# Transposes of the folded spectrum moved into the same round's other small matmuls, in front of them

## The chip, the cores and the metric

The kernel runs on one core of one Trainium2 chip. The metric is the device time of one execution in microseconds; lower is better. The three runs of the kernel before took 1345.86, 1345.98 and 1347.0 us.

## The reference

Three stages follow each other on an input of 4 batches x 3136 positions x 256 channels, all in float32:

```python
y = irfft(rfft(x, axis=1) * (filt_r + 1j * filt_i), n=3136, axis=1)      # filter along the positions
m = real(fft(fft(y, axis=1), axis=2))                                    # spectrum along both axes
u = y + m
u = u + relu(norm(u) @ w1a) @ w2a                                        # 256 -> 1024 -> 256
u = u + relu(norm(u) * g @ w1b) @ w2b                                    # again, with a gain
```

`norm` subtracts the mean over the channels and divides by the root of the variance plus 1e-6.

## The kernel before

**The products.** Almost all of TensorE's work is the two channel products. The tokens come in 25 units U of 512 tokens (the last has 256), each with two layers. A block (U, layer) has eight steps, so there are 400 steps. A step has a first product (`w1_step`, line 904: 12 matmuls of 256 columns, from `xth` and `xtl`, the high and low half of the normalised tokens) and a second (`w2_step`, line 931: 8 matmuls with `hh`, then 4 with `hl`). Between them `w1_evict` makes `hh` (ScalarE, line 913) and `hl` (VectorE, line 914). The main loop (lines 1110 to 1121) does, for step i: the first product of step i + 2, then all that the table `at` holds for step i, then the second product of step i, then the eviction of step i + 2. So whatever `at` calls on TensorE interrupts the products at one fixed place, after line 904 of step i + 2 and ahead of line 931 of step i. Every engine works through its instructions in the order written here.

**The filter beside them.** Batch 0's filter runs ahead of the products. For batches 1 to 3 it runs in pieces under the products of the batch before: `over_p(b)` (first transform), then `over_q(b)`, a generator whose `yield`s divide it into ticks. Its main loop runs over rounds j = 0 to 9, each with two ticks, in two neighbouring steps (`slots`; `first` puts the tick ahead of all else at its step). A round does, for frequency pair group j and the group before it:

- `into(j)`: 64-row matmuls from `gr` into two PSUM banks R and I (line 267, `ps<-gr`);
- `back(j - 1)`: 64-row matmuls from the filtered `y` into two banks V (line 267, `ps<-y`), which ScalarE copies to `vst` (line 609; in round 1 line 605, and VectorE's 606);
- `filt(j, R, I)`: four VectorE multiplications with the filter (line 573), then two GpSimd additions (lines 574 and 575) that make `y`;
- `turn_z(j - 1)`: four transposes of `z` by TensorE (line 618; two in the last round), copied by ScalarE to `zt` (line 625);
- `half(j)`: GpSimd folds `y` into `z` (line 584, two instructions), ScalarE sets its first column (line 585);
- `store`, `sign`, `load_g`, `load_f`: the output of V, a sign for the next filter, the next loads.

The first four rounds' steps of batch 1 are 25, 30, 34 and 36; rounds 5 and 6 stand at 50 and 52. In batches 2 and 3 rounds are five or more steps apart, at steps that leave 4, 9 or 14 when divided by 16. At those that leave 4 the tick is followed by the split of a coming block's `xtl` (line 825, VectorE; line 824, ScalarE, makes `xth`).

**Normalisation.** `ln_ticks` makes `xth` and `xtl`. Most blocks turn the tokens through DRAM (`TURN`); the first units, the last ones and each batch's first unit turn them on TensorE (lines 828 to 838): per half k of the channels four transposes (line 831), a copy by ScalarE and a split by VectorE, and a `yield`. Of these, eight blocks have the two halves at two different steps: layer 0 of units 6, 12, 18 and 24, layer 1 of units 1, 2, 23 and 24. In the others both ticks fall into one step.

PSUM has eight banks, all from one pool (`bank`); two hold the sums of the second product.

Of the kernel before, what the change touches and what calls it, by code (L numbers as in the profile page):

```python
# [13 lines left out]
ACTF = mybir.ActivationFunctionType  # L14
ALU = mybir.AluOpType
# [168 lines left out]
def spectral_mlp_kernel(ctx: ExitStack, tc, x, ff, ff0, cst, w1a, w2a, gln, w1b, w2b, out):  # L184
# [43 lines left out]
    def bank(k=1):  # L228
        t = banks.tile([128, 512], F32, tag="b", name="ps")
        return t if k == 1 else t.rearrange("p (a d) -> p a d", a=k)  # L230

    def f32(ap):
        return ap.bitcast(F32)
# [28 lines left out]
    def split(src, hi, lo, lo_eng=None):  # L262
        nc.scalar.activation(out=hi, in_=src, func=ACTF.Copy)
        (lo_eng or nc.vector).tensor_tensor(out=lo, in0=src, in1=f32(hi), op=ALU.subtract)
# [264 lines left out]
    def over_q(b):  # L529
# [17 lines left out]
        def into(j):  # L547
            g = g_raw.pop((b, j))
            R, I = (bank(2) for _ in range(2))
            f2 = const("f2")  # L550
            if j == 0:
                for r, o, n in ((0, R, "f2a"), (64, I, "f2a")):
                    quarter(o[:, 0], 0, const(n), r, NI, g[:, 0])
                for r, o, n in ((0, I, "f2b"), (64, R, "f2b")):
                    quarter(o[:, 0], 64, const(n), r, NI, g[:, 0])
                for r, o in ((0, R), (64, I)):
                    quarter(o[:, 1], 0, f2, r, NI, g[:, 1])
                for r, o in ((0, I), (64, R)):
                    quarter(o[:, 1], 64, f2, r, NI, g[:, 1])
            else:  # L560
                n = len(steps_of(j))
                for c in range(2):
                    for r, o in ((0, R), (64, I)):
                        quarter(o[:, :n], 64 * c, f2, r, NI, g[:, c:2 * n:2])
            return R, I
# [22 lines left out]
        def back(j):  # L588
            n = len(steps_of(j))
            y = ys.pop(j)  # L590
            V = [bank(2) for _ in range(2)]
            if j == 0:
                for c in range(2):
                    for h in range(2):
                        quarter(V[h][:, 0], 64 * c, const("i1z", 64 * c, 64), 64 * h, NQ, y[:, 0, c])
                for c in range(2):
                    quarter(V[0][:, 1], 64 * c, const("i1", 64 * c, 64), 0, NQ, y[:, 1, c])
            else:
                for c in range(2):
                    for h in range(2):  # L600
                        quarter(V[h][:, :n], 64 * c, const("i1", 64 * c, 64), 64 * h, NQ, y[:, :n, c])
            st = stg.tile([128, 4, D], F32, tag="st", name="vst")
            vst[j] = st
            if j == 0:
                nc.scalar.activation(out=st[:, :2], in_=V[0], func=ACTF.Copy)
                nc.vector.tensor_tensor(out=st[:, 0], in0=V[1][:, 0], in1=st[:, 0], op=ALU.add)
            else:
                for h in range(2):
                    nc.scalar.activation(out=st[:, h:2 * n:2], in_=V[h][:, :n], func=ACTF.Copy)
# [21 lines left out]
        sign(0)  # L631
        yield
        for j in range(NDUO + lag):
            RI = into(j) if j < NDUO else None
            if j >= lag:
                back(j - lag)
            if RI:
                filt(j, *RI)
            yield
            if j >= lag:  # L640
                turn_z(j - lag)
            i = j - lag + 1
            if 0 <= i < NDUO:
                half(i)
            if j >= lag:
                store(j - lag)
            if j + 1 < NDUO:
                sign(j + 1)
            if j + 2 < NDUO:
                load_g(b, j + 2)  # L650
            nxt = j + 2
            if nxt < NDUO:
                load_f(b, nxt)
            yield
# [107 lines left out]
    def ln_ticks(U, layer, sets=None):  # L762
        n = tiles(U)
        u = u_of[U]
        xs = {}
        turn = (U, layer) in TURN
        xall = None
        for tl in sets or [slice(0, n)]:
            ts = range(n)[tl]
            scaled = U < 2 or turn  # L770
            st = sm.tile([128, 4, 6], F32, tag="bs", name="bs")
            mv = sm.tile([128, 4, 2], F32, tag="mv", name="mv")
            rs = sm.tile([128, 4], F32, tag="rs", name="rs")
            for t in ts:
                nc.vector.bn_stats(out=st[:, t], in_=u[:, t])  # L775
            for t in ts:
                nc.vector.bn_aggr(out=mv[:, t], in_=st[:, t])
            nc.vector.tensor_scalar_add(out=rs[:, tl], in0=mv[:, tl, 1], scalar1=EPS)  # L778
            nc.gpsimd.tensor_tensor(out=rs[:, tl], in0=rs[:, tl], in1=mhalf[:, tl], op=ALU.pow)  # L779
            yield  # L780
            if scaled:
                nb = sm.tile([128, 4], F32, tag="nb", name="nb")
                nc.vector.scalar_tensor_tensor(out=nb[:, tl], in0=mv[:, tl, 0], scalar=-1.0, in1=rs[:, tl],  # L783
                                               op0=ALU.mult, op1=ALU.mult)
            xall = xall or xnp.tile([128, 4 * D], F32, tag="xn", name="xn")
            for t in ts:
                xs[t] = xall[:, t * D:t * D + D]
                if turn:
                    xs[t] = xall.rearrange("p (j k t a) -> p j k t a", j=4, k=2, t=4)[:, :, :, t]
                    nc.scalar.activation(out=xs[t], in_=u[:, t].rearrange("p (k a j) -> p j k a", k=2, j=4),  # L790
                                         func=ACTF.Identity, scale=rs[:, t:t + 1], bias=nb[:, t:t + 1])
                    if t % 2:
                        yield
                    continue
                if scaled:
                    nc.scalar.activation(out=xs[t], in_=u[:, t], func=ACTF.Identity, scale=rs[:, t:t + 1],
                                         bias=nb[:, t:t + 1])
                    continue
                nc.vector.tensor_scalar(out=xs[t], in0=u[:, t], scalar1=mv[:, t, 0:1], scalar2=rs[:, t:t + 1],
                                        op0=ALU.subtract, op1=ALU.mult)  # L800
        if turn:


            nc.vector.transpose(out=xall, in_=xall)
            xd = xdp.tile([128, 4 * D], F32, tag="xd", name="xd")
            nc.sync.dma_start(out=xd, in_=xall)
        yield
        xt = {s: xtp.tile([128, 2, 512], F32R, tag="x" + s, name="xt" + s) for s in "hl"}
        xt_of[U, layer] = xt
        w = n * 128  # L810
        if turn:
            src = xd.rearrange("(i a) (j c r) -> i (a j) c r", i=4, j=4, c=8)
            dst = f32(xt["l"]).rearrange("p k (t i r) -> i p (k t) r", t=4, i=4)
            for i in range(4):
                nc.sync.dma_start(out=dst[i], in_=src[i])
            yield
            for k in range(2):
                h, l = (xt[s][:, k] for s in "hl")
                if layer:
                    nc.scalar.activation(out=h, in_=f32(l), func=ACTF.Copy, scale=g_sb[:, k:k + 1])  # L820
                    nc.vector.scalar_tensor_tensor(out=l, in0=f32(l), scalar=g_sb[:, k:k + 1], in1=f32(h),
                                                   op0=ALU.mult, op1=ALU.subtract)
                else:
                    nc.scalar.activation(out=h, in_=f32(l), func=ACTF.Copy)
                    nc.vector.tensor_tensor(out=l, in0=f32(l), in1=f32(h), op=ALU.subtract)  # L825
                yield
            return
        for k in range(2):
            ps = bank()
            for t in xs:  # L830
                nc.tensor.transpose(ps[:, t * 128:t * 128 + 128], xs[t][:, k * 128:k * 128 + 128], ident)  # L831
            if layer:
                nc.scalar.activation(out=xt["h"][:, k, :w], in_=ps[:, :w], func=ACTF.Copy, scale=g_sb[:, k:k + 1])
                nc.vector.scalar_tensor_tensor(out=xt["l"][:, k, :w], in0=ps[:, :w], scalar=g_sb[:, k:k + 1],  # L834
                                               in1=f32(xt["h"][:, k, :w]), op0=ALU.mult, op1=ALU.subtract)
            else:
                split(ps[:, :w], xt["h"][:, k, :w], xt["l"][:, k, :w])
            yield

    alone = False  # L840
# [108 lines left out]
    with tc.manual_schedule():  # L949
# [60 lines left out]
        k = 0  # L1010
# [197 lines left out]
```

## Time and profile before

| | |
|---|---|
| three runs, us | 1345.86, 1345.98, 1347.0 (median 1345.98) |
| the profiled execution, us | 1346.94 |
| its span from the first to the last instruction, us | 1345.2 |
| TensorE, matmuls | 1317.5 us busy, 98% of the span |
| VectorE | 796.5 us, 59% |
| ScalarE | 616.9 us, 46% |
| GpSimd | 270.5 us, 20% |
| mean granted TensorE clock | 0.992 |

The profiled execution lies 0.96 us above the median; 1.74 us of it lie outside the span. TensorE's matmuls overlap in the records, so its busy time says that it is the bound, not how much of it is lost; that is read from the starts of its instructions in the timeline.

### The profile page before, as it was taken

To read this page: it belongs to the slowest core of one execution; us is meant where nothing else is said; L and a number is where in the kernel's file an instruction comes from. 1 tells how busy PE (TensorE), PEld (TensorE's weight loads), DVE (VectorE), ACT (ScalarE), POOL (GpSimd) and SP (SyncE) were. 2 spreads that over 40 slices of the span, in tenths; PEclk is the share of its full clock that TensorE was granted. 3 is DMA by queue.
4 is the path that set the end of the run, shared out by engine and by line. 5 is a ranking of instruction groups with operands and counts; after the bars stand their busy time and mean duration, and the time that the engine had idled before them with its cause. 6 is when DMAs were issued, how large, how long until landed. Compare 5 with 4: busy or idle time off the path is not lost.

```text
span 1345.2 us, 27766 instructions
## 1 busy us (share of the span) xinstructions
PE 1317.5 (98%) x11221; PEld 1211.0 (90%) x11221; DVE 796.5 (59%) x1643; ACT 616.9 (46%) x1205; POOL 270.5 (20%) x277
## 2 busy tenths in 40 slices
PE   8969999999999999999999999999999999999998
PEld 6527998899989989999988999999999999999998
DVE  5968875666454666656454665656555555465453
ACT  5646544454435444544434544545434443444322
POOL 1763012332040222212032221312000000000000
PEclk9979999999999999999999999999999999999999
DMA  8754323443544634623353535534221413332200
GB/s 315 253 192 146 101 92 76 154 115 86 134 140 136 153 91 116 165 62 95 89 170 104 161 106 123 147 81 111 56 64 48 95 34 77 80 83 45 64 17 24
DMA packets 214920, 147.97 MB, mean 110 GB/s; under 512 B 163516, under 2 KB 187196, under 8 KB 214792
## 3 DMA queue, kind: packets, MB, share of 16 engines
q1 hardware_dynamic: 198056, 117.36, 33.6%
q10 hardware_dynamic: 16736, 28.84, 5.9%
q8 instruction: 88, 1.44, 0.5%
q14 instruction: 40, 0.33, 0.1%
HBM read 87.71 MB, written 58.46 MB: 109 GB/s over the span
## 4 chain that ended last, share of the span: by engine, by line
PE 92%; DVE 4%; DMA 1%; ACT 1%; issue 1%; POOL 1%; SPq 0%; ACTq 0%; DVEq 0%; POOLq 0%
PE ps L931 39%; PE ps L904 38%; PE ps L267 7%; PE ps L731 2%; PE ps L320 2%; PE ps L365 1%; PE ps L426 1%; PE ps L618 1%; PE ps L831 1%; PE ps L382 0%; DVE hl L914 0%; DMA vd<-vst 0%; DVE bs L775 0%; DMA gd<-gst 0%; DVE wm L873 0%
## 5 line engine op out<-in xcount | busy, mean ns | idle before, releaser
L914 DVE SCALAR_TENSOR_TENSOR hl<-ps,hh 128x512 fp32r<-128x512 f32 (+1 forms) x400 | 269.5, 675 | 328.6 <-ACT hh L913 323.1
L913 ACT ACTIVATE hh<-ps 128x512 fp32r<-128x512 f32 (+1 forms) x400 | 233.6, 586 | 359.1 <-PE ps L931 314.9
L904 PE MATMUL ps<-xth,w1a 128*128 128x256 f32 x1568 | 243.0, 276 | 0.0
L904 PE MATMUL ps<-xth,w1b 128*128 128x256 f32 x1568 | 242.5, 276 | 0.0
L931 PE MATMUL ps<-w2a,hh 128*128 128x256 f32 x1568 | 219.5, 282 | 0.0
L931 PEld LDWEIGHTS ps<-w2a,hh 128*128 128x128 f32 x1568 | 194.4, 189 | 27.0 <-issue 24.6
L931 PE MATMUL ps<-w2b,hh 128*128 128x256 f32 x1568 | 215.1, 279 | 0.5 <-ACT hh L913 0.5
L904 PEld LDWEIGHTS ps<-xth,w1a 128*128 128x128 f32 x1568 | 207.9, 188 | 1.3 <-issue 1.3
L904 PEld LDWEIGHTS ps<-xth,w1b 128*128 128x128 f32 x1568 | 207.5, 188 | 0.0
L931 PEld LDWEIGHTS ps<-w2b,hh 128*128 128x128 f32 x1568 | 193.2, 188 | 15.4 <-issue 13.8
L779 POOL TENSOR_TENSOR rs<-rs,mhalf 128x4 f32<-128x4 f32 (+1 forms) x51 | 50.9, 997 | 591.6 <-DVE rs L778 506.6
L904 PE MATMUL ps<-xtl,w1a 128*128 128x256 f32 x784 | 154.6, 277 | 0.0
L904 PE MATMUL ps<-xtl,w1b 128*128 128x256 f32 x784 | 154.3, 276 | 0.0
L790 ACT ACTIVATE xn<-u,nb,rs 128x256 f32<-128x256 f32 x152 | 120.3, 840 | 49.5 <-DVE nb L783 47.6
L931 PE MATMUL ps<-w2b,hl 128*128 128x256 f32 x784 | 122.0, 277 | 1.3 <-DVE hl L914 1.3
L931 PE MATMUL ps<-w2a,hl 128*128 128x256 f32 x784 | 121.9, 277 | 1.1 <-DVE hl L914 1.1
L904 PEld LDWEIGHTS ps<-xtl,w1a 128*128 128x128 f32 x784 | 118.7, 188 | 0.6 <-DVE xtl L825 0.6
L904 PEld LDWEIGHTS ps<-xtl,w1b 128*128 128x128 f32 x784 | 118.7, 188 | 0.2 <-DVE xtl L834 0.2
L931 PEld LDWEIGHTS ps<-w2b,hl 128*128 128x128 f32 x784 | 103.8, 188 | 2.1 <-DVE hl L914 2.1
L931 PEld LDWEIGHTS ps<-w2a,hl 128*128 128x128 f32 x784 | 104.2, 188 | 1.3 <-DVE hl L914 1.3
L935 DVE TENSOR_TENSOR u<-ps,u 128x512 f32<-128x512 f32 x98 | 63.1, 685 | 44.4 <-PE ps L931 44.4
L775 DVE BATCH_NORM_STATS2 bs<-u 128x6 f32<-128x256 f32 x196 | 68.6, 411 | 0.0
(146 smaller groups left out, 1449.1 us busy)
## 6 DMA issues: line engine op xcount, KB each, us to landing
xd<-xn SPq DMA_DIRECT2D x38, 512.0 KB
xtl<-xd SPq DMA_DIRECT2D x152, 128.0 KB
fc<-in_ff SPq DMA_DIRECT2D x34, 512.0 KB
vr<-vd SPq DMA_DIRECT2D x48, 256.0 KB
out<-u SPq DMA_DIRECT2D x24, 512.0 KB
vd<-vst ACTq DMA_DIRECT2D x21, 512.0 KB
xr<-in_x SPq DMA_DIRECT2D x18, 512.0 KB
gd<-gst ACTq DMA_DIRECT2D x36, 256.0 KB
```

What stands on the lines that cost most here:

```text
L267: nc.tensor.matmul(out=o[c:c + 64], lhsT=lhs[r:r + k], rhs=rhs[r:r + k], **{"start": True, "stop": True, **kw})
L320: nc.tensor.matmul(out=o, lhsT=cf[at // 512][:k, at % 512:at % 512 + w], rhs=rhs[:k, c0:c1], start=start, stop=stop)
L365: nc.tensor.matmul(out=ps[:, o:o + 128], lhsT=x[:, j, a * 128:a * 128 + 128], rhs=cf[0][:, :128], start=True, stop=True)
L731: nc.tensor.matmul(out=ps[a][:, eo], lhsT=lhs, rhs=cs[eo][r], start=eo == 1 and i == 0, stop=False, skip_group_check=True)
L775: nc.vector.bn_stats(out=st[:, t], in_=u[:, t])
L779: nc.gpsimd.tensor_tensor(out=rs[:, tl], in0=rs[:, tl], in1=mhalf[:, tl], op=ALU.pow)
L790: nc.scalar.activation(out=xs[t], in_=u[:, t].rearrange("p (k a j) -> p j k a", k=2, j=4), func=ACTF.Identity, scale=rs[:, t:t + 1], bias= ...
L904: nc.tensor.matmul(out=ps[:, c:c + 256], lhsT=w[:, a, k, m * 128:m * 128 + 128], rhs=xt[s][:, k, c:c + 256], start=i == 0, stop=i == len(t ...
L913: nc.scalar.activation(out=h[:, :n], in_=ps[:, :n], func=ACTF.Relu)
L914: nc.vector.scalar_tensor_tensor(out=l[:, :n], in0=ps[:, :n], scalar=0.0, in1=f32(h[:, :n]), op0=ALU.max, op1=ALU.subtract)
L931: nc.tensor.matmul(out=o[:, t % 2], lhsT=a[:, t * 128:t * 128 + 128], rhs=w[:, b, m], start=m == 0 and i == 0 and t % 2 == 0, stop=m == 7 ...
L935: nc.vector.tensor_tensor(out=u[:, t - 1:t + 1], in0=o, in1=u[:, t - 1:t + 1], op=ALU.add)
```

## The change

In a round, the transposes of the group before (`turn_z`) leave the second tick and go to the first, ahead of `back`; `back` now stands ahead of `into`. In the normalisation, every unit but the first turns both halves of the channels in one tick: eight transposes into two banks, then the two pairs of copies and splits. The second tick of those that had one is then empty.

```diff
         for j in range(NDUO + lag):
-            RI = into(j) if j < NDUO else None
-            if j >= lag:
-                back(j - lag)
-            if RI:
-                filt(j, *RI)
-            yield
             if j >= lag:
                 turn_z(j - lag)
+                back(j - lag)
+            if j < NDUO:
+                filt(j, *into(j))
+            yield
             i = j - lag + 1
             if 0 <= i < NDUO:
                 half(i)
...
-        for k in range(2):
-            ps = bank()
-            for t in xs:
-                nc.tensor.transpose(ps[:, t * 128:t * 128 + 128], xs[t][:, k * 128:k * 128 + 128], ident)
-            if layer:
...
-            else:
-                split(ps[:, :w], xt["h"][:, k, :w], xt["l"][:, k, :w])
+        for ks in ((0, 1),) if U else ((0,), (1,)):
+            out_k = {k: bank() for k in ks}
+            for k, ps in out_k.items():
+                for t in xs:
+                    nc.tensor.transpose(ps[:, t * 128:t * 128 + 128], xs[t][:, k * 128:k * 128 + 128], ident)
+            for k, ps in out_k.items():
+                if layer:
...
+                else:
+                    split(ps[:, :w], xt["h"][:, k, :w], xt["l"][:, k, :w])
             yield
```

From here on the changed kernel's lines below 631 carry other numbers (the transposes of line 831 are at line 830, `xtl` of line 825 at line 823).

TensorE at round 6 of batch 1 (steps 52 and 53), before: `gr` is read by `into`, `y` by `back`, `z` by `turn_z`.

```order
L904 MATMUL ps<-xtl,w1b 128x256 x2
L267 MATMUL ps<-gr,con 64x512 x4
L267 MATMUL ps<-y,con 64x512 x4
L931 MATMUL ps<-w2b,hh 128x256 x8
L931 MATMUL ps<-w2b,hl 128x256 x4
L904 MATMUL ps<-xth,w1b 128x256 x4
L904 MATMUL ps<-xtl,w1b 128x256 x2
L904 MATMUL ps<-xth,w1b 128x256 x4
L904 MATMUL ps<-xtl,w1b 128x256 x2
L618 MATMUL ps<-con,z 128x128 x4
L931 MATMUL ps<-w2b,hh 128x256 x8
```

And in the changed kernel:

```order
L904 MATMUL ps<-xtl,w1b 128x256 x2
L618 MATMUL ps<-con,z 128x128 x4
L267 MATMUL ps<-y,con 64x512 x4
L267 MATMUL ps<-gr,con 64x512 x4
L931 MATMUL ps<-w2b,hh 128x256 x8
```

The trace shows each of the 64-row matmuls of line 267 as two instructions, so x4 here is x8 there. The transposes stand one step earlier, and `into` stands last in its interruption instead of first. There are 27 such rounds with `turn_z`, 24 of them with an `into`.

ScalarE in the round at step 41 of batch 1, before (the `zt` copies stand in the second tick):

```order
L913 ACTIVATE hh<-ps 128x512
L609 ACTIVATE vst<-ps 128x2x256 x2
L913 ACTIVATE hh<-ps 128x512
L625 ACTIVATE zt<-ps 128x8x49
L585 ACTIVATE z<-y 128x4
L545 DMA vd<-vst 128x1024
```

And in the changed kernel:

```order
L913 ACTIVATE hh<-ps 128x512
L625 ACTIVATE zt<-ps 128x8x49
L609 ACTIVATE vst<-ps 128x2x256 x2
L913 ACTIVATE hh<-ps 128x512
L585 ACTIVATE z<-y 128x4
L545 DMA vd<-vst 128x1024
```

The copy of the transposes moves ahead of the copies of V; the store's DMA keeps its place. VectorE, GpSimd and the DMA queue of SyncE keep their order in the rounds.

## Rows read from the trace of the kernel before

**Rows 1.** The page, part 1: busy time, share of the span, instructions.
```profile
PE 1317.5 (98%) x11221; PEld 1211.0 (90%) x11221; DVE 796.5 (59%) x1643; ACT 616.9 (46%) x1205; POOL 270.5 (20%) x277
```

**Rows 2.** Timeline, TensorE, step 132: start us, us, engine, line, operation, tiles, form, count.
```profile
552.24 1.09 PE L267 MATMUL ps<-gr,con 50*64 50x512 f32 x8
553.15 1.04 PE L267 MATMUL ps<-y,con 49*64 49x512 f32 x8
554.12 1.18 PE L931 MATMUL ps<-w2b,hh 128*128 128x256 f32 x8
...
556.95 0.60 PE L618 MATMUL ps<-con,z 128*128 128x128 f32 x4
557.31 1.17 PE L931 MATMUL ps<-w2b,hh 128*128 128x256 f32 x8
558.31 0.62 PE L931 MATMUL ps<-w2b,hl 128*128 128x256 f32 x4
...
559.90 0.39 PE L904 MATMUL ps<-xtl,w1a 128*128 128x256 f32 x2
...
560.13 1.07 PE L931 MATMUL ps<-w2b,hh 128*128 128x256 f32 x8
...
561.03 0.62 PE L931 MATMUL ps<-w2b,hl 128*128 128x256 f32 x4
```

**Rows 3.** Timeline, TensorE, the last round of batch 1 with two transposes.
```profile
343.08 0.38 PE L618 MATMUL ps<-con,z 128*128 128x128 f32 x2
...
344.23 0.62 PE L931 MATMUL ps<-w2b,hl 128*128 128x256 f32 x4
```

**Rows 4.** Timeline, TensorE, batch 0: transposes followed by 64-row matmuls.
```profile
80.58 0.44 PE L454 MATMUL ps<-con,z 128*128 128x128 f32 x2 [2.39 <-ACT z L477]
80.95 1.41 PE L267 MATMUL ps<-xf,con 64*64 64x512 f32 x8
```

**Rows 5.** Timeline, VectorE, step 132; then the view of line 825 alone.
```profile
553.38 0.69 DVE L573 TENSOR_TENSOR y<-ps,fc 128x512 f32<-128x512 f32 x1 [1.05 <-PE ps L267]
...
555.88 3.02 DVE L825 TENSOR_TENSOR xtl<-xtl,xth 128x512 fp32r<-128x512 f32 x2
```
```profile
L825 DVE TENSOR_TENSOR xtl<-xtl,xth x36: 680/1319/1782, 239.2 to 1244.5; 128x512 fp32r<-128x512 f32 x36
```

**Rows 6.** Timeline, batch 1, rounds 5 and 6 (steps 50 to 52).
```profile
290.22 1.43 POOL L584 TENSOR_TENSOR z<-y 128x254 f32<-128x254 f32 x2
```
```profile
292.50 0.59 ACT L913 ACTIVATE hh<-ps 128x512 fp32r<-128x512 f32 x1
```
```profile
291.45 1.09 PE L267 MATMUL ps<-gr,con 50*64 50x512 f32 x8
```

**Rows 7.** Timeline, batch 1, rounds 2 and 3 (steps 34 to 38).
```profile
233.33 1.43 POOL L584 TENSOR_TENSOR z<-y 128x254 f32<-128x254 f32 x2
...
235.57 1.09 PE L267 MATMUL ps<-gr,con 50*64 50x512 f32 x8
...
239.21 3.08 DVE L825 TENSOR_TENSOR xtl<-xtl,xth 128x512 fp32r<-128x512 f32 x2
...
244.00 0.69 DVE L914 SCALAR_TENSOR_TENSOR hl<-ps,hh 128x512 fp32r<-128x512 f32 x1
...
244.74 0.74 PE L931 MATMUL ps<-w2b,hl 128*128 128x256 f32 x4 [0.21 <-DVE hl L914]
```

**Rows 8.** Timeline, batch 1, round 1 (steps 30 to 33).
```profile
216.04 0.68 DVE L573 TENSOR_TENSOR y<-ps,fc 128x512 f32<-128x512 f32 x1
...
221.45 1.19 PE L931 MATMUL ps<-w2b,hh 128*128 128x256 f32 x8 [0.32 <-ACT hh L913]
...
224.66 1.19 PE L931 MATMUL ps<-w2b,hh 128*128 128x256 f32 x8 [0.20 <-ACT hh L913]
```

**Rows 9.** Timeline, batch 2, step 110 and after: ScalarE and TensorE.
```profile
488.09 0.59 ACT L913 ACTIVATE hh<-ps 128x512 fp32r<-128x512 f32 x1
...
490.01 1.07 PE L931 MATMUL ps<-w2b,hh 128*128 128x256 f32 x8
```

More of the change, by code (lines that the diff above doesn't have):

```diff
@@ L827, in ln_ticks @@
             return
-        for k in range(2):
-            ps = bank()
-            for t in xs:
-                nc.tensor.transpose(ps[:, t * 128:t * 128 + 128], xs[t][:, k * 128:k * 128 + 128], ident)
-            if layer:
-                nc.scalar.activation(out=xt["h"][:, k, :w], in_=ps[:, :w], func=ACTF.Copy, scale=g_sb[:, k:k + 1])
-                nc.vector.scalar_tensor_tensor(out=xt["l"][:, k, :w], in0=ps[:, :w], scalar=g_sb[:, k:k + 1],
-                                               in1=f32(xt["h"][:, k, :w]), op0=ALU.mult, op1=ALU.subtract)
-            else:
-                split(ps[:, :w], xt["h"][:, k, :w], xt["l"][:, k, :w])
+        for ks in ((0, 1),) if U else ((0,), (1,)):
[5 more added lines that the diff above has]
+                if layer:
+                    nc.scalar.activation(out=xt["h"][:, k, :w], in_=ps[:, :w], func=ACTF.Copy, scale=g_sb[:, k:k + 1])
+                    nc.vector.scalar_tensor_tensor(out=xt["l"][:, k, :w], in0=ps[:, :w], scalar=g_sb[:, k:k + 1],
+                                                   in1=f32(xt["h"][:, k, :w]), op0=ALU.mult, op1=ALU.subtract)
+                else:
+                    split(ps[:, :w], xt["h"][:, k, :w], xt["l"][:, k, :w])
             yield
```

## Prediction

> **What bounds the kernel now.** I read the busy times first, then TensorE's timeline around the interruptions, then the timelines of the engines that feed it. TensorE is busy for 98% of the span [rows 1], no other engine for more than 59%. The timeline shows that this is not an average over idle and full stretches: once the filter runs under the products, TensorE goes from product to small matmul and back without waiting, but for a few rows that carry an idle time in brackets. So two things count: how long TensorE itself takes for what it issues, and whether anything it needs comes later than before. The change touches both.
>
> **TensorE's own saving.** Eight products take 560.13 to 561.03 = 0.90 us [rows 2]. With four transposes ahead of them, it is 556.95 to 558.31 = 1.36 us, so that interruption costs 0.46 us. With two transposes it is 343.08 to 344.23 = 1.15 us [rows 3], so 0.25 us. Two more transposes cost 0.21 us, one about 0.11 us. Four at 0.11 us are 0.43 to 0.44 us, and what is left, 0.02 to 0.03 us, is the price of the interruption as such. That alone is what a joined interruption can give back; the transposes stay. The changeover that the trace lacks at full load is transposes to 64-row matmuls. The nearest row is from batch 0: two transposes and the changeover take 80.58 to 80.95 = 0.37 us after a wait [rows 4]; less two paces of 0.11 us, the changeover adds 0.15 us at most beyond a transpose's own pace. A round also begins with a changeover today, so the difference lies between 0.05 us worse and 0.05 us better. I take 0.02 us saved for each of 27 rounds and as much for each of the eight border blocks: 35 x 0.02 = **0.7 us saved**, with ends at 1.8 us saved and 1.4 us lost (27 x 0.05).
>
> Here a rule speaks for the change. The Trainium skill (TensorE: Matmul & The Clock Gate, "Back-to-back issue gap") gives a lone matmul of N columns a spacing of N / 2.4 + 2.5 ns at the full clock, so 56 ns for 128 columns; an estimate by it is 0.22 us for four transposes, and 0.24 us of the 0.46 us would be the interruption. The same section says that the formula leaves out the weight loads. The rows decide against it here: the third and fourth transpose cost as much as the first two.
>
> The border blocks also move the second half's copy and split one to three steps earlier. Their inputs are ready at the first half's step, so nothing new is waited for; the copies join other work on ScalarE and VectorE, which have room. I cost that at nothing.
>
> **What the filter loses.** Now `into` comes after the transposes and `back`. The four multiplications (line 573) wait for it. At step 132 they start at 553.38, 1.14 us after `into` began at 552.24 [rows 2, 5]. In the changed kernel `into` begins later by four transposes (0.44 us) and by `back`, as long as the 0.91 us from 552.24 to 553.15: **1.35 us later**. All that follows them on VectorE moves too, and so do GpSimd's additions and `half`. TensorE's own schedule hardly moves: 0.44 us more in this interruption, 0.46 us less in the next. So every slack below 1.35 us behind `filt` becomes a wait of TensorE.
>
> *Six rounds ahead of an `xtl` split* (steps 116, 132, 148, 212, 228, 244). The two splits of line 825 follow the multiplications directly, 555.88 to 558.90 [rows 5]; TensorE wants the second at 559.90 [rows 2]. Slack 1.00 us, delay 1.35 us: 0.35 us of waiting, and some 0.05 us to restart. 6 x 0.4 = **2.4 us lost**. The ends: one split takes 0.68 us at least and 1.78 us at most [rows 5], so the pair could take 1.36 us, which leaves no wait, or 3.56 us, 0.5 us more each: 0 to 5.4 us.
>
> The long splits run beside GpSimd's additions. The Trainium skill (SBUF — State Buffer, "Who interferes with whom") says that a VectorE instruction with two SBUF inputs and a GpSimd instruction that reads SBUF shut each other out for a whole instruction, the later one waiting. The spread of line 825 from 0.68 to 1.78 us agrees; as both streams are moved by the same 1.35 us, I leave the overlap as it is.
>
> *Batch 1, round 5 to 6.* The rounds stand two steps apart. GpSimd's two instructions of `half` end at 291.65 [rows 6]; they move by 1.35 us, so `z` is complete at 293.0. The transposes now head round 6, due about 0.1 us ahead of today's 291.45 as they need no changeover; the second of them, due at 291.45, needs the second `half`. That is a wait of **1.6 us**; `turn_z` used to come one step later. All eight PSUM banks are then in use, and bank I is the one that the transposes just left, free when ScalarE has copied it. ScalarE's `hh`, 292.50 to 293.09 today [rows 6], waits behind a normalisation that waits for the same GpSimd queue, so it ends near 294.45, and a copy of half a microsecond near 294.95; `into` wants I at 293.0 + 0.33 (the transposes) + 0.2 (changeover) + 0.91 (`back`) = 294.45 and so waits **0.45 us**. The split of `xtl`, later still, adds 0.15 us. Together **2.2 us lost**.
>
> *Batch 1, round 2 to 3.* The same, without the other GpSimd work between. `half` ends at 234.76 [rows 7], so at 236.1 in the change; the second transpose is due at about 235.57: **0.6 us**. The multiplications of round 3 follow 1.9 us later than today, the splits end at 242.29 + 1.9 = 244.2, and `hl`, which VectorE makes next but for the statistics of a normalisation, ends at 244.69 + 1.9 = 246.6. TensorE waits for that `hl` already today, at 244.74, so it moves by the whole **1.9 us**, the 0.6 us included.
>
> *Four rounds ahead of a normalisation* (steps 110, 126, 206, 222). Here the multiplications delay the bias, the bias two ScalarE normalisations, and these `hh`: 488.09 to 488.68, wanted at 490.01 [rows 9], slack 1.33 us. With 1.35 us it is just late, and the next `hh` too; I take 0.2 us each: **0.8 us lost**, 0 to 2 us.
>
> *Round 1 of batch 1 gains.* VectorE must first finish line 606, which waits for `back`; so the multiplications start only at 216.04 [rows 8]. With `back` first, `into` is done at about 215.57, 0.47 us earlier, and the copies of the transposes leave ScalarE's queue between. TensorE idles 0.32 and 0.20 us for `hh` behind it; I take **0.5 us saved**. The remaining rounds (first, last, and those that leave 9 by 16) have more slack than 1.35 us behind them, or no `filt`.
>
> The store's DMA, the loads on SyncE's queue and GpSimd's order keep their places; `store` waits for copies of V that now come earlier.
>
> **The sum.** -0.7 + 2.4 + 2.2 + 1.9 + 0.8 - 0.5 = +6.1 us. On the profiled execution, 1346.94 us, that is 1353.0; on the median of the runs, 0.96 us lower, 1345.98 + 6.1 = **1352.1 us**, 0.45% slower.
>
> **The rivals.** *The delay is absorbed.* If line 825 runs without GpSimd beside it, and `half` overlaps better than the rows say, no new wait reaches TensorE and only 0.7 us of saving remains: 1345.3. For it: VectorE idles over a third of the time. Against: rows 5 to 7 stand in the very stretches where it does not. 0.17.
>
> *The interruption is dearer than I read, and the change is faster.* After transposes the eight products take 557.31 to 558.31 = 1.00 us, 0.10 us more than otherwise [rows 2]. If that were the interruption's and not the last transpose's, 35 x 0.10 = 3.5 us come back: 1342.5, as long as the waits stay below that. The point that decides is whether the joined rounds cost less than 2.34 us (1.88 + 0.46). Against it speaks the comparison of two and four transposes. By the formula of the Trainium skill named above, the estimate would be 35 x 0.24 = 8.4 us. 0.07.
>
> *Banks run short in every round.* A joined interruption takes five banks where it took four. If not two but all 24 rounds waited some 0.5 us, as in round 6, the cost would be 12 us on top of the sum less the 0.45 us counted: 1364. Against it: only in the two close rounds does the order make a bank wait for an eviction of the same interruption. 0.07.
>
> **The numbers.** My forecast has 0.69. A measurement of this kernel can tell about 0.2%, 2.7 us, from no change. The forecast and the bank rival are slower: 0.76. The absorbed delay is the same; 0.17. The dearer interruption is faster: 0.07. The range: the lost terms at their lower ends (splits 0, normalisation 0) give 1349, and the absorbed case 1345.3; upward, the splits' upper end adds 3 us, the normalisations' 1.2 us and the changeover 2 us: 1358. I give 1345.0 to 1358.0; outside lie the faster case, the bank rival and a little of both ends.
>
> **What would show it.** Right: in the profile after, transposes, `y` and `gr` matmuls in one row of 2.32 us; line 573 about 2.5 us after the interruption's start; idle rows of TensorE named for `xtl` line 823 after the six rounds, and for `z` (GpSimd, line 584) at steps 36 and 52 of batch 1. Wrong: no such idle rows, or eight products after a joined round in 0.90 us and a shorter interruption; idle rows at line 267 in most rounds would be the bank rival.

## The result, and the profile after

The changed kernel takes 1357.76 us (median of five runs, 1356.48 to 1358.47) against 1345.96 us (five runs, 1345.31 to 1347.0): a ratio of 1.0086, with a 95% interval of 1.0072 to 1.0101. It is 11.8 us slower; 6.1 us were forecast. The new waits are there, each close to its size in the sum, and they explain rather less than half of the loss. The larger part is in no wait.

The page, part 1, of the changed kernel; it answers to [rows 1]:

```profile
PE 1327.3 (98%) x11221; PEld 1216.6 (90%) x11221; DVE 796.4 (59%) x1643; ACT 618.3 (46%) x1205; POOL 270.9 (20%) x277
```

The counts are those of before. TensorE is busy 9.8 us longer with the same instructions, a first sign that not all of the loss is waiting: but for waits inside a row, idle time does not count as busy. The mean granted clock is 0.991 (0.992 before).

TensorE's timeline, step 132 and after, changed kernel (start us, us, line, tiles, form, count; the idle time and its releaser in brackets); it answers to [rows 2]:

```profile
554.80 0.40 PE L904 MATMUL ps<-xtl,w1b 128*128 128x256 f32 x2
555.03 0.60 PE L618 MATMUL ps<-con,z 128*128 128x128 f32 x4
555.56 1.09 PE L267 MATMUL ps<-y,con 49*64 49x512 f32 x8
556.47 1.04 PE L267 MATMUL ps<-gr,con 50*64 50x512 f32 x8
557.44 1.20 PE L931 MATMUL ps<-w2b,hh 128*128 128x256 f32 x8
558.48 0.62 PE L931 MATMUL ps<-w2b,hl 128*128 128x256 f32 x4
...
560.29 1.07 PE L931 MATMUL ps<-w2b,hh 128*128 128x256 f32 x8
561.20 0.62 PE L931 MATMUL ps<-w2b,hl 128*128 128x256 f32 x4
...
562.33 0.62 PE L904 MATMUL ps<-xth,w1a 128*128 128x256 f32 x4
563.14 0.50 PE L904 MATMUL ps<-xtl,w1a 128*128 128x256 f32 x2 [0.19 <-DVE xtl L823]
563.48 1.10 PE L931 MATMUL ps<-w2b,hh 128*128 128x256 f32 x8
564.42 0.64 PE L931 MATMUL ps<-w2b,hl 128*128 128x256 f32 x4
564.89 0.63 PE L904 MATMUL ps<-xth,w1a 128*128 128x256 f32 x4
```

Three things are to be read here. *The interruption:* from the two products ahead of it to the end of the eight behind it, 554.80 to 558.48 = 3.68 us. Two and eight products without an interruption take 0.23 + 0.91 us (560.29 to 561.20 for the eight), so it costs 2.54 us. For the kernel before, the same is measured between these rows of its timeline and those of [rows 2]:

```profile
551.92 0.39 PE L904 MATMUL ps<-xtl,w1b 128*128 128x256 f32 x2
...
555.13 0.62 PE L931 MATMUL ps<-w2b,hl 128*128 128x256 f32 x4
...
556.72 0.40 PE L904 MATMUL ps<-xtl,w1b 128*128 128x256 f32 x2
```

551.92 to 555.13 = 3.21 us, 2.07 us more than the products; 556.72 to 558.31 = 1.59 us, 0.45 us more. Together 2.52 us: to the rounding of the rows, joining saves nothing. In the medians over all such rounds (3.67 us joined, 3.21 and 1.59 us apart, less 1.13 us for ten products) it saves 0.01 us. *The wait:* `xtl` is late at 563.14, as forecast. *The pace:* eight products take 0.91 us before that wait and 563.48 to 564.42 = 0.94 us after it. That last difference is small, and it lasts for 80 us.

VectorE in the same stretch, changed kernel; it answers to [rows 5]:

```profile
557.56 0.69 DVE L573 TENSOR_TENSOR y<-ps,fc 128x512 f32<-128x512 f32 x1 [1.93 <-PE ps L267]
...
559.97 3.12 DVE L823 TENSOR_TENSOR xtl<-xtl,xth 128x512 fp32r<-128x512 f32 x2
```

The multiplications start 2.53 us after the interruption (1.14 us before), and the two splits end at 563.09. TensorE, undisturbed, would have taken the second at 562.78.

TensorE at round 6 of batch 1 (step 52), changed kernel; it answers to [rows 6]:

```profile
291.48 0.33 PE L618 MATMUL ps<-con,z 128*128 128x128 f32 x1 [0.78 <-POOL z L584]
292.16 0.55 PE L618 MATMUL ps<-con,z 128*128 128x128 f32 x3 [0.36 <-POOL z L584]
292.64 1.09 PE L267 MATMUL ps<-y,con 49*64 49x512 f32 x8
293.55 1.51 PE L267 MATMUL ps<-gr,con 50*64 50x512 f32 x8
294.99 1.18 PE L931 MATMUL ps<-w2b,hh 128*128 128x256 f32 x8
```

Both halves of `z` are late here, and the `gr` matmuls take 1.44 us to the next start instead of 0.97: the wait for bank I, 0.47 us, inside their row.

The pace shows in the view by line. First the kernel before, from step 134 to step 158 (560 to 639 us), then the changed kernel over the same steps (563 to 645 us); columns: count, busy us and mean ns of one, idle time before:

```profile
L904 PE MATMUL ps<-xth,w1a 128*128 128x256 f32 x121 | 18.8, 276 | 0.0
...
L904 PE MATMUL ps<-xth,w1b 128*128 128x256 f32 x72 | 11.1, 276 | 0.0
```

```profile
L904 PE MATMUL ps<-xth,w1a 128*128 128x256 f32 x120 | 19.0, 281 | 0.0
...
L904 PE MATMUL ps<-xth,w1b 128*128 128x256 f32 x72 | 11.4, 281 | 0.0
```

A matmul of 276 ns stands for a start every 113.3 ns, one of 281 ns for a start every 118 ns. The clock that was granted is the same at both, 1.00, the upper of its two levels (2.4 GHz); stretches of the changed kernel at the slower and then at the faster pace (us, length, busy time and count of line 904's matmuls, granted clock, DMA share, GB/s):

```profile
564.00:644.00 80.00, 37.97 (x288) 1.00 0.36 96
646.00:700.00 54.00, 27.40 (x216) 1.00 0.46 128
```

There is hardly a spacing between the two: TensorE runs a whole stretch at the one pace or at the other, and changes only at an interruption or a wait. Of some 9,300 pairs of neighbouring products, 475 stand 117 to 125 ns apart in the trace of before and 2131 in that of the changed kernel (larger distances are waits). The long slow stretches there are 563 to 645 us and 877 to 958 us (578 products each, both from the wait for `xtl` two steps after a round), 342 to 380 us behind batch 1's last round (312 products) and 1309 to 1334 us behind the joined border transposes of unit 23's layer 1 (210). At 4.6 ns each these four hold 7.7 us; before, the longest has some 120 products.

**The account.** I take the start of every step's second product in both traces, from step 20 (the start-up before it varies from trace to trace, by -1.8 to +2.3 us) to the last step. "Pace" is the sum, over neighbouring products up to 125 ns apart, of what exceeds 113.3 ns; "waits" is the rest. All in us, against the trace of before; the last column counts slow pairs from step 20 on (334 before).

| kernel | median less before's | from step 20 | pace | waits | slow pairs |
|---|---|---|---|---|---|
| changed | +11.8 | +12.6 | +7.3 | +5.3 | 1979 |
| changed, run again | +11.4 | +12.4 | +6.0 | +6.3 | 1682 |
| border units alone | +1.2 | +0.8 | +1.4 | -0.6 | 655 |
| swap alone | +4.5 | +3.1 | +2.7 | +0.4 | 933 |
| `z` last | +14.4 | +12.1 | +15.6 | -3.5 | 3866 |
| four lone transposes | +12.6 | +12.7 | +5.3 | +7.4 | 1513 |
| filter behind the splits | +8.0 | +5.7 | +3.1 | +2.6 | 1037 |
| `z`, `into`, `back` | +5.1 | +4.6 | +3.1 | +1.5 | 1039 |
| `z`, `into`, `back`, behind | +4.4 | +4.3 | +3.4 | +0.9 | 1118 |
| `into`, `z`, `back` | +14.7 | +13.7 | +7.0 | +6.7 | 1909 |

### The profile page after: what moved, and what is told of

Read it like the earlier page. It is cut to its first block, busy times and chain, and to the rows that moved or that the text cites. A ratio compares the mean times of both kernels' runs of the same rounds, so it can differ in the third digit from the quotient of the medians.

```text
span 1355.9 us, 27732 instructions
## 1 busy us (share of the span) xinstructions
PE 1327.3 (98%) x11221; PEld 1216.6 (90%) x11221; DVE 796.4 (59%) x1643; ACT 618.3 (46%) x1205; POOL 270.9 (20%) x277
## 3 DMA queue, kind: packets, MB, share of 16 engines
q8 instruction: 88, 1.44, 0.4%
## 4 chain that ended last, share of the span: by engine, by line
PE 92%; DVE 4%; DMA 1%; POOL 1%; issue 1%; ACT 1%; SPq 0%; ACTq 0%; DVEq 0%; POOLq 0%
PE ps L931 38%; PE ps L904 38%; PE ps L267 7%; PE ps L729 2%; PE ps L320 2%; DVE xtl L823 1%; PE ps L365 1%; PE ps L618 1%; PE ps L426 1%; DVE t L573 1%; PE ps L830 1%; PE ps L382 0%; DMA vd<-vst 0%; DVE y L573 0%; DVE hl L914 0%
```

## The experiments

Two theories stood against each other. **Lateness:** `into` ends its interruption, so the filter is 1.35 us late, and TensorE waits for what follows; a joined order in which `into` isn't late loses nothing. **Pace:** joined rounds, or the waits, leave TensorE at the slower pace. Each edit is against the changed kernel.

**Border units alone.** The round as in the kernel before; the normalisation's two halves joined.

```diff
+            RI = into(j) if j < NDUO else None
             if j >= lag:
-                turn_z(j - lag)
                 back(j - lag)
-            if j < NDUO:
-                filt(j, *into(j))
+            if RI:
+                filt(j, *RI)
             yield
+            if j >= lag:
+                turn_z(j - lag)
```

> The rounds as before; only the border units' eight transposes in one tick. My theory (the loss is the filter's lateness plus a slower pace of the products, both from the rounds) gives no change: within 1 us of the kernel before, joined border interruptions of 0.90 to 0.92 us where two of 0.45 us stood. A rival, that the border units' copies crowd ScalarE and VectorE and make the loss, gives 3 us or more above before.

Measured: 1347.75 us, ratio 1.0008 (0.9999 to 1.0018). So as a time this part makes no difference that can be told. Its trace does show one long slow stretch, behind the eight `xn` transposes of unit 23's layer 1, 210 products long, which the changed kernel has too. Four matmuls of `w2a` take 0.47 us in it; 0.45 is the other pace:

```profile
1300.50 0.63 PE L933 MATMUL ps<-w2a,hh 128*128 128x256 f32 x4
1300.97 0.40 PE L933 MATMUL ps<-w2a,hl 128*128 128x256 f32 x2
```

That isn't chance: in all nine traces of kernels with joined border units, this interruption was entered at the faster pace and left at the slower one; in the two without (the kernel before and `into`, `z`, `back`) its two halves left the faster pace as it was. At 4.6 ns a product it is 1.0 us, which the interval of this run allows.

**Swap alone.** `back` ahead of `into`, `turn_z` in the second tick as before.

```diff
             if j >= lag:
-                turn_z(j - lag)
                 back(j - lag)
             if j < NDUO:
                 filt(j, *into(j))
             yield
+            if j >= lag:
+                turn_z(j - lag)
```

> As the changed kernel, but the transposes of z stay alone in the second tick; back still stands ahead of into. The filter starts 0.91 us later than before instead of 1.35. Lateness: the six xtl splits have 1.00 us, so no wait there; round 3 of batch 1 about 1.3 us, round 1 half a microsecond gained: 1346 to 1348 us. Pace: if a lone set of transposes brings the products back to 113 ns, as 27 of 27 did before, few products run at 118 ns (below 700) and nothing is added. If ending an interruption with into is what sets the slow pace, over 2000 products at 118 ns and 7 us more: 1353 to 1356.

Measured: 1351.07 us, ratio 1.0029 (1.0018 to 1.0041). `into` is late by `back` alone. The swap, with the border units that this kernel keeps, costs 4.5 us of the 11.8, in the trace mostly by pace. Time and slow pairs (997 in the whole trace) both lie between the two cases of the expectation, so it decides for neither.

**`z` last.** All three in one interruption, `into` first, so nothing behind the filter is late.

```diff
+            RI = into(j) if j < NDUO else None
             if j >= lag:
-                turn_z(j - lag)
                 back(j - lag)
-            if j < NDUO:
-                filt(j, *into(j))
+                turn_z(j - lag)
+            if RI:
+                filt(j, *RI)
```

> The round in one interruption, ordered into, back, transposes: the filter starts when it did before, the interruption ends with transposes. Lateness theory: no new waits. Pace theory: transposes at the end leave 113 ns. Together 1345 to 1347 us. If joining as such costs (five banks, a changeover more), each of 24 rounds costs more than 2.54 us and the time is above 1350.

Measured: 1360.96 us, ratio 1.0102 (1.0081 to 1.0123), the worst but one. The waits went as expected (the column is 3.5 us below the kernel before); the pace took 15.6 us. TensorE's timeline of this kernel at step 132:

```profile
556.00 0.39 PE L905 MATMUL ps<-xtl,w1b 128*128 128x256 f32 x2
556.32 1.09 PE L267 MATMUL ps<-gr,con 50*64 50x512 f32 x8
557.23 1.04 PE L267 MATMUL ps<-y,con 49*64 49x512 f32 x8
558.20 0.66 PE L618 MATMUL ps<-con,z 128*128 128x128 f32 x4
558.61 1.19 PE L932 MATMUL ps<-w2b,hh 128*128 128x256 f32 x8
559.64 0.63 PE L932 MATMUL ps<-w2b,hl 128*128 128x256 f32 x4
...
561.52 1.10 PE L932 MATMUL ps<-w2b,hh 128*128 128x256 f32 x8
562.47 0.63 PE L932 MATMUL ps<-w2b,hl 128*128 128x256 f32 x4
```

The interruption is the cheapest of all, 556.00 to 559.64 = 3.64 us where the changed kernel takes 3.68 us, and the next eight products take 0.95 us. All nine such rounds that were entered at the faster pace were left at the slower one; of 15 entered at the slower pace, seven kept it. My expectation that transposes at the end would leave TensorE at the faster pace fell here, and with it the theory that lateness is all: the filter isn't late in this order, and it loses more. The time is above 1350, but not because a round is dearer.

**Four lone transposes.** The changed kernel with work added: at steps 136, 152, 232 and 248 four transposes of the identity into a bank that nobody reads.

```diff
+        def scratch():
+            ps = bank()
+            for t in range(4):
+                nc.tensor.transpose(ps[:, t * 128:t * 128 + 128], ident, ident)
+
+        for w in (136, 152, 232, 248):
+            call(w, scratch)
```

> The changed kernel with four transposes of the identity added alone, into a bank that nobody reads, at steps 136, 152, 232 and 248: work added. By themselves they cost 4 x 0.46 = 1.8 us. Pace theory: they bring the products after them from 118 back to 113 ns; products at 118 ns fall from 2131 to about 900, 5 us come back, so 3 us faster than the changed kernel: about 1354.5. If the pace is set by buffers or banks and not by what interrupts the products, 1.8 us slower: about 1359.5, and the count stays near 2100.

Measured: 1359.13 us, ratio 1.0086 (1.0058 to 1.0114). The time is that of the second case (1359.5), but it decides nothing, since in its trace the slow stretches behind the rounds at steps 132 and 228 hadn't formed. Where TensorE was slow when it met the added transposes (two of the four places), they changed its pace:

```profile
623.07 0.64 PE L931 MATMUL ps<-w2b,hl 128*128 128x256 f32 x4
623.54 0.63 PE L904 MATMUL ps<-xth,w1a 128*128 128x256 f32 x4
...
624.96 0.60 PE L1050 MATMUL ps<-con 128*128 128x128 f32 x4
...
626.32 0.62 PE L931 MATMUL ps<-w2a,hl 128*128 128x256 f32 x4
626.77 0.62 PE L904 MATMUL ps<-xth,w1a 128*128 128x256 f32 x4
```

Four products take 0.47 us ahead of line 1050 and 0.45 us behind it. In the kernel before all 27 lone groups of `z` transposes were entered and left at the faster pace. But two cases are few: in this same trace all three ordinary joined rounds (those with an `into`, but for each batch's second, which has other shapes) that were entered at the slower pace were left at the faster one too, and in the trace of the border units alone the one lone group of `z` that was entered slow (218 us) was left slow.

**Filter behind the splits.** The round's ticks of batches 2 and 3 stand behind all else at their steps; TensorE's order is that of the changed kernel.

```diff
-                    first(w, q)
+                    (first if b == 1 else put)(w, q)
```

> The changed kernel with one word changed in batches 2 and 3: a round's tick comes behind what else its step holds, so VectorE splits xtl and sets the normalisation's bias ahead of the filter's multiplications. TensorE's instructions keep their order. Lateness theory: the six xtl waits (2.5 us) and the waits behind the normalisations (0.7 us) go. If the long slow stretches of batches 2 and 3 begin at the xtl waits, as the changed kernel's trace suggests, they go as well, up to 5 us more: 1349 to 1351 us, under 1000 products at 118 ns. If the joined order by itself sets the slow pace, only 3 us come back and over 2000 products stay at 118 ns: about 1354.5.

Measured: 1354.71 us, ratio 1.0061 (1.0046 to 1.0076), 3.5 us below the changed kernel run beside it. VectorE at step 132 of this kernel, and the waits of TensorE for `xtl` over the whole run (us in total, times, longest) here and then in the changed kernel:

```profile
559.55 1.29 DVE L823 TENSOR_TENSOR xtl<-xtl,xth 128x512 fp32r<-128x512 f32 x2 [0.84 <-ACT xth L822]
561.07 0.69 DVE L573 TENSOR_TENSOR y<-ps,fc 128x512 f32<-128x512 f32 x1 [0.22 <-PE ps L267]
```

```profile
PE ps L904 <- DVE xtl L823: 0.4, 2, 0.2
```

```profile
PE ps L904 <- DVE xtl L823: 1.2, 6, 0.3
```

The splits now run before the multiplications and free of GpSimd's additions, which follow those: 1.29 us for two, 3.12 us in the changed kernel. The waits behind the six rounds are gone, and with them the slow stretches that began there: all 21 ordinary joined rounds were entered and left at the faster pace. So one edit that removes no interruption takes away a part of the waits and a part of the pace. What the pace still costs, 3.1 us, is for the most part the stretches behind batch 1's last round and behind unit 23, which this kernel shares with the changed one (2.4 us). A new wait came with the edit, once: at step 229 the copy `zt` now stands behind `xth`, which waits for a load, and TensorE idles 1.12 us for it.

The time is that of the expectation's second case (1354.5), the slow pairs (1092 in the whole trace) are near those of its first. The two traces differ by some 6.6 us from step 20 on, the runs by 3.5 us: the start-up, which the edit doesn't touch, is 3.2 us longer in this trace. How much of the 6.6 us other executions get is not shown.

**`z`, `into`, `back`.** `into` in the middle, late by the transposes alone.

```diff
             if j >= lag:
                 turn_z(j - lag)
+            RI = into(j) if j < NDUO else None
+            if j >= lag:
                 back(j - lag)
-            if j < NDUO:
-                filt(j, *into(j))
+            if RI:
+                filt(j, *RI)
```

> The round in one interruption, ordered transposes, into, back: the filter 0.44 us later than before, round 6 of batch 1 still waits for z, some 0.9 us; no xtl wait, as 0.44 is below 1.00 us. Pace: 23 of 23 interruptions of into and back that ended with back left 113 ns; if that end is what counts, few slow products (below 700) and 1346 to 1348 us. If joining transposes and 64-row matmuls in one interruption is what lets a slow pace in, as with the transposes last, over 2000 slow products and 1353 or more.

Measured: 1351.79 us, ratio 1.0039 (1.0024 to 1.0054). Of the waits 1.5 us stay, mostly at step 52, where the transposes still meet an unfinished `z`. Time and slow pairs (1104) lie between the two cases of the expectation.

**`z`, `into`, `back`, behind the splits.** The last two edits together.

```diff
             if j >= lag:
                 turn_z(j - lag)
+            RI = into(j) if j < NDUO else None
+            if j >= lag:
                 back(j - lag)
...
-                    first(w, q)
+                    (first if b == 1 else put)(w, q)
```

> The two together: transposes, into, back in one interruption, and in batches 2 and 3 the tick behind the step's other work. No wait of the rounds is left but batch 1's. If the pace stays at 113 ns it is the best of the joined orders, 1345 to 1347 us; if joining brings the slow pace, no better than the same order without the second edit.

Measured: 1351.1 us, ratio 1.0031 (1.0019 to 1.0043). The lowest time of the joined orders, though by no more than the runs of one kernel scatter (0.7 us), and still slower than the kernel before. The hope of 1345 to 1347 us fell.

**The changed kernel again,** on the same chip as the last three, with its own trace.

> The changed kernel once more, beside these on one chip. The waits must stand at the same steps with the same lengths (six xtl waits of 0.35 to 0.45 us, 1.0 us for z at step 52 of batch 1). If the slow pace is a state that a wait may or may not leave behind, its stretches move and their sum differs from the 2131 products of the first profile by several hundred; if it belongs to the program's buffers, it is the same count.

Measured: 1358.18 us, ratio 1.0090 (1.0072 to 1.0108). The time repeats, its make-up less so. TensorE waits for `xtl` behind the same six rounds, and for `z` at step 52 by 0.77 and 0.35 us (0.78 and 0.36 us in the first trace). The slow pairs are 1757 where the first trace had 2131, and they stand elsewhere. Between 820 and 876 us the same line reads as follows, first in the changed kernel's trace, then in this one:

```profile
L904 PE MATMUL ps<-xth,w1a 128*128 128x256 f32 x69 | 10.7, 276 | 0.0
```

```profile
L904 PE MATMUL ps<-xth,w1a 128*128 128x256 f32 x64 | 10.1, 280 | 0.0
```

The same program runs this stretch at either pace. So the pace isn't fixed by its addresses or its order alone; it is a state that TensorE is in. (On which chip the first trace was taken is not on record; but within each trace, too, the same wait behind different rounds leaves either pace.)

**`into`, `z`, `back`.** `into` first, transposes in the middle, and the kernel before's border units.

```diff
+            RI = into(j) if j < NDUO else None
             if j >= lag:
                 turn_z(j - lag)
                 back(j - lag)
-            if j < NDUO:
-                filt(j, *into(j))
+            if RI:
+                filt(j, *RI)
...
```

> The kernel before (border units too), with the transposes joined into the first tick between into and back: into first, so the filter is not late; back last. Lateness theory: no new xtl wait, z at step 52 due 0.9 us later than in the changed kernel and ready, so no new wait at all. Pace: interruptions that ended with back left 113 ns in 23 of 23 before and 20 of 21 in the order transposes, into, back, so few slow products (below 700). With the transposes last, the trace lost 15.6 us to the pace and was 3.5 us shorter in all else; if that is the joining's own gain, this order shows it: 1343 to 1346 us. If transposes joined to 64-row matmuls let the slow pace in wherever they stand, over 2000 slow products and 1350 or more.

Measured: 1360.99 us, ratio 1.0119 (1.0102 to 1.0136), the worst. TensorE's timeline of this kernel at step 132:

```profile
556.47 0.40 PE L903 MATMUL ps<-xtl,w1b 128*128 128x256 f32 x2
556.80 1.09 PE L267 MATMUL ps<-gr,con 50*64 50x512 f32 x8
557.82 0.65 PE L618 MATMUL ps<-con,z 128*128 128x128 f32 x4
558.40 1.09 PE L267 MATMUL ps<-y,con 49*64 49x512 f32 x8
559.42 1.19 PE L930 MATMUL ps<-w2b,hh 128*128 128x256 f32 x8
560.45 0.62 PE L930 MATMUL ps<-w2b,hl 128*128 128x256 f32 x4
```

556.47 to 560.45 = 3.98 us, 0.30 us more than in the changed kernel; in 24 rounds 7.2 us, about the 6.7 us of "waits" in the table. Transposes between two groups of 64-row matmuls are dearer than at either end of them.

Of the expectation's cases the second came: 1986 slow pairs, though `back` ends each interruption. But the pace is regular here. Of the 21 ordinary rounds 12 were entered at the faster pace, and all 12 were left at the slower one; nine were entered at the slower pace, and all nine were left at the faster one. Every one of them changed it. The two stretches on either side of the round above:

```profile
L903 PE MATMUL ps<-xth,w1b 128*128 128x256 f32 x44 | 7.0, 281 | 0.0
```

```profile
L903 PE MATMUL ps<-xth,w1a 128*128 128x256 f32 x32 | 4.9, 276 | 0.0
```

The first is 541 to 556 us, the second 561 to 573 us.

## Why the prediction came out as it did

The direction held, and so did the mechanism of the waits, but the forecast is half of the loss. That the range still holds the time, by 0.24 us, is luck: its upper end was made of longer splits, later normalisations and a dearer changeover, none of which came, and not of what did come. Point by point, from the moves of each step's start:

| term | forecast us | measured us |
|---|---|---|
| TensorE's own saving | -0.7 | -0.2 (0.01 a round, in the medians) |
| six waits for `xtl` | +2.4 | +2.5 (0.46, 0.47, 0.34, twice over) |
| batch 1, round 5 to 6 | +2.2 | +2.2 (2.04 at step 52, 0.20 at 54) |
| batch 1, round 2 to 3 | +1.9 | +1.9 (0.55 at step 36, 1.32 at 38) |
| four normalisation rounds | +0.8 | +0.7 (0.13 or 0.14, five times) |
| round 1 of batch 1 | -0.5 | -0.75 |
| the pace of the products | not in the sum | +7.3 |

- **The saving.** The joined round was to take less than 2.34 us to its products if the change was to win. It took 557.44 - 555.03 = 2.41 us, and the eight products behind it 1.04 us. So the rival of the dearer interruption is out: the eight products take 1.04 us behind the joined interruption, 1.01 and 1.00 us behind the two apart, so nothing comes back. Again the rows speak against the formula for a lone matmul in the Trainium skill (TensorE: Matmul & The Clock Gate, "Back-to-back issue gap"), by which the estimate was that 8.4 us come back.
- **The delay.** 1.35 us was read from the length of `back` and of the transposes; the multiplications start 2.53 - 1.14 = 1.39 us later in their interruption. The slack was read at one place of each kind and held for the others, and each kind gave its wait. The experiments bear this out: with `into` first (`z` last), or with the splits ahead of the multiplications, those waits are gone.
- **The splits.** I left their overlap with GpSimd as it was. That was right for the change (3.02 us before, 3.12 us after). The run that moved them out of it shows what the overlap costs: 1.29 us for the pair alone. That agrees with the Trainium skill (SBUF — State Buffer, "Who interferes with whom"), by which a VectorE instruction with two inputs in SBUF contends with a GpSimd instruction that reads SBUF.
- **Border units.** Costed at nothing but eight small savings. Alone they add 1.2 us (-0.1 to 2.4), no difference that can be told; but the slow stretch behind unit 23 comes with them in each trace, 1.0 us that the sum doesn't have.
- **Bank rival.** Only step 52 waits for a bank, by 0.47 us. The absorbed delay is out too.
- **A gain that I missed.** At step 77 TensorE waited for `xf` in the kernel before (its eight matmuls took 1.82 us to the next start, 1.02 us in the changed one). The late TensorE no longer meets that wait: 0.7 us back. With it the terms of the table without the pace come to some 5.7 us, the "waits" of the account to 5.3 us.

**The step that failed** is the first: "Eight products take 0.90 us" was taken from one place and held for the whole run, so that the sum has no term for the pace of the products. In the trace of before it holds for all but 475 pairs. The changed kernel has 1645 more slow pairs from step 20 on, at some 4.5 ns each, and they are the 7.3 us that the sum lacks. Part of them hangs on the waits that I did forecast: without the waits for `xtl` (filter behind the splits) the pace costs 3.1 us instead of 7.3 us, and in the two traces of the changed kernel six of the ten such waits behind the six rounds that began at the faster pace left the slower one. How long a slow stretch lasts then differs: of the ordinary joined rounds entered slow, six of seven were left slow in the first trace of the changed kernel, two of five in the second and none of three with the four lone transposes.

**What stays open** is what in TensorE sets the pace at the end of an interruption. It isn't the kind of matmul that ends it alone: of the interruptions entered at the faster pace, `z` last leaves 9 of 9 slow, the lone `z` transposes of the kernel before none of 27, its `xn` transposes 2 of 17. It isn't the program alone either, since two executions of one program differ. Yet it isn't without order. The `into` of each batch's first round, alone in its interruption, was entered at the faster pace 31 times in the eleven traces and left TensorE slow all 31 times; the two times that it was entered slow, it left TensorE fast. In `into`, `z`, `back` every ordinary round changes the pace. In the changed order 68 of 69 ordinary rounds entered at the faster pace kept it (four traces). So some interruptions change the pace and others keep it; what distinguishes them, no run here shows. Shown are the slower pace, what it costs, and the places named here at which it begins. That lone transposes end it is not shown.

## What to carry to other kernels

Joining two interruptions of a stream saves only the price of an interruption as such, here 0.01 us of 0.46 in the changed order and 0.04 us with the transposes last; work it out from two interruptions of different length before anything is moved for it. What has a long tail behind it on other engines goes first in its interruption: list the slack of each consumer and set the delay against it, which here gave every wait to within 0.3 us. And compare the pace of the main stream itself, in several stretches, not only its waits: 4.5 ns in a matmul's spacing was the larger half of this loss, in rows that show no idle time at all.

## What the runs showed of the hardware

- Products of 256 columns run at one of two paces, a start every 113.3 ns or every 118 ns (276 or 281 ns in the records), with the granted clock at 1.00 (2.4 GHz, the upper level) in both; a pace lasts until an interruption or a wait, up to 578 products in the changed kernel, and can differ between two executions of one program.
- Some interruptions change the pace each time: 64-row `into` matmuls alone 33 of 33 times, `into`, transposes, `back` 21 of 21 times.
- Four transposes add 0.45 us ahead of the 64-row matmuls and 0.42 us behind them to an interruption of 3.21 us, and 0.78 us between them (medians over the rounds, measured from the two products ahead to the end of the eight behind).
- Two VectorE subtractions of 128x512 with both inputs in SBUF took 1.29 us with GpSimd idle, and 3.02 and 3.12 us beside its additions.
